# Output weights of a scan made over two temporaries in an idle buffer, with their loads first in the queue and new planner seeds

## The chip, the cores and the metric

The kernel runs on one core of one Trainium2 chip. The metric is device time in microseconds (us). Before the change three runs took 769.33, 770.93 and 770.23 us, a median of 770.23 us. A core has five engines that are named here as in the profile: PE (matrix multiply; PEld is its weight load), ACT (activation functions), DVE (vector), POOL (GpSimd) and SP, which only issues DMAs. Each engine runs its own list of instructions in order, and they wait for each other through semaphores.

## The reference, cut to what matters

Two branches, whose results stand side by side in the output (2048 rows, 640 + 640 columns).

```python
# A: a diagonal complex state-space scan
dt = jnp.exp(log_dt)
Lam_bar = jnp.exp(dt * Lam)
B_bar = ((Lam_bar - 1.0) / Lam)[:, None] * Bmat
Bu = jnp.einsum("bld,pd->blp", x + 0j, B_bar)
for t in range(L):
    h = Lam_bar[None, :] * h + Bu[:, t, :]
y = 2.0 * jnp.einsum("blp,dp->bld", hseq, Cmat).real + x * Dskip
# B: attention with 32 query heads of 20 columns over one key and one value head
scores = jnp.einsum("bhqd,bkd->bhqk", q, k) * (Dh ** -0.5)
p = softmax(scores, axis=-1)
out = jnp.einsum("bhqk,bkd->bhqd", p, v) @ wo
```

S = L = 2048, D = P = 640.

## The kernel before

**Attention sets the pace.** The 2048 query rows are four blocks of 512, the 32 heads go in groups of four, so there are 32 groups. A group needs its scores against 16 key chunks for each of four heads: 64 units of 128 keys x 512 query columns, 2048 units in all. A unit goes one of two ways. Either PE writes its scores into one of two large PSUM tiles, `R0` (three units) or `R1` (two units), and one ACT instruction (L1263, here "an exp") takes two or three units at a time to `P`; or PE writes them into a single bank, and DVE approximates the exponential in integers: one conversion (L1269) and three shifted copies (L1274) over up to three units at once (here "a D unit"). PE then multiplies the exponentials with the values into `PV`, DVE takes a finished group out (`OTr`, L1307), SP stores it to `o_rows`. Four times, after eight groups, `dense_ops` reads a whole block back into `OTd`, POOL multiplies it by the softmax denominators, and PE projects it with `WO4`. A group takes at most 16 D units (`QUOTA`).

**The scan runs in between.** It has four blocks of 512 rows and five chunks of 128 states, 20 scan units. For each, PE multiplies the input (`xaT`) with `BTre` and `BTim`, DVE rotates the result (`tm0` to `tm3`, L901), POOL adds it up (`uh`, L917), DVE runs the recurrence (`hh`, L928), POOL rotates back (`tm4` to `tm7`) and adds up into `W`. When the five chunks of a block are there, `y_tile` multiplies `W` with the output weights `CGre` and `CGim`.

**The output weights** are C scaled per state by a complex factor that is made on the chip: for each of the five chunks and each of re and im, POOL makes a product in five pieces of 128 columns in the temporary `ctmp` (L858), and DVE makes the other product and the sum in one instruction (L860). C arrives by transposing DMAs into buffers that are idle so far: chunks 0 to 3 lie in `W`, chunk 4 in `ostage`. `ctmp` lies in `tm4` to `tm6`. So the way back of the scan, which writes `tm4` to `tm7`, is gated until all ten weights are made (`prog["c"]`).

**A planner sets the order.** Nothing is ordered by hand after the set-up: at build time `main` keeps the remaining operations in named threads (`sc` holds what precedes the scan, its DMAs among it; `sa`, `su`, `sr`, `sy` are the scan; `sx` loads `xaT` of the later blocks), offers the head of every thread beside the next exp, fill, D unit and so on, and issues what can begin first by the planner's own durations, with small random choices. The choices are varied over 64 equal stretches of the 2048 units, each with a seed from `SEEDS` (0 is a seed like another). The order that comes out is fixed in the program: each engine runs its list, and an instruction that waits holds up everything behind it on its engine. A gate is tested when the planner issues, not on the chip; there only semaphores wait.

Of the kernel before, what the change touches and what calls it, by code (L numbers as in the profile page):

```python
# [9 lines left out]
ALU = mybir.AluOpType  # L10
AX = mybir.AxisListType
FP32 = mybir.dt.float32
# [231 lines left out]
class _Kernel:  # L244
    S, D, H, DH = 2048, 640, 32, 20
    NC, NQB, NKC, NGG = 5, 4, 16, 8
# [18 lines left out]
    SEEDS = (19006, 20002, 21006, 22006, 23001, 24003, 25001, 26002, 27008, 28003, 0, 30006, 31008, 32005, 33006,  # L265
# [28 lines left out]
    def alloc(self):  # L294
        S, NC = self.S, self.NC
# [66 lines left out]
        self.ctmp = self.tm[:].rearrange("p i n -> p (i n)").bitcast(FP32)[:, 1024:1664]  # L362
# [454 lines left out]
    def scan_ops(self):  # L817

        K, NC = self, self.NC
        sc, NGRE, NGIM, GRE, GIM = K.sc, self.NGRE, self.NGIM, self.GRE, self.GIM  # L820
        t = self.t
        sa, su, sr, sy, sc_ = [], [], [], [], []
        self.prog = prog = dict(x=0, a=0, u=0, s=0, r=0, y=0, w=0, c=0)
# [9 lines left out]
        ct = [f"tm{i}{h}" for i in (4, 5, 6) for h in self.PIECES]  # L833
# [14 lines left out]
        for c in range(NC):  # L848
            for i, nm in ((0, "cre"), (1, "cim")):
                sc_.append(self.dma(K.Craw[c][:, i, :], t[nm][:, 128 * c:128 * (c + 1)], f"craw{c}{i}",  # L850
                                    writes=[f"Craw{c}{i}"] + ([f"ostage{i}"] if c == 4 else []), tr=True, kb=160))
        for c in range(NC):
            cr, ci = K.Craw[c][:, 0, :], K.Craw[c][:, 1, :]
            keys = [f"Craw{c}0", f"Craw{c}1", "sc"] + (["ostage0", "ostage1"] if c == 4 else ws)
            for (dst, x, y, gx, gy, op, nm) in ((K.CGre, cr, ci, GRE, GIM, ALU.subtract, "CGre"),
                                                (K.CGim, ci, cr, NGRE, NGIM, ALU.add, "CGim")):
                for i in range(0, 640, 128):
                    pool(lambda e, y=y, c=c, gy=gy, i=i: e.tensor_scalar(K.ctmp[:, i:i + 128], y[:, i:i + 128], sc[:, gy, c:c + 1],  # L858
                                                                         None, op0=ALU.mult), keys, [f"ct{i}"] + ct * (i == 0), 128)
                dve(lambda e, dst=dst, x=x, op=op, c=c, gx=gx: e.scalar_tensor_tensor(  # L860
                    out=dst[:, c, :], in0=x, scalar=sc[:, gx, c:c + 1], in1=K.ctmp, op0=ALU.mult, op1=op),
                    keys + ct + [f"ct{i}" for i in range(0, 640, 128)], [nm], 695)
        sc_[-1].done = lambda: prog.update(c=1)
        for b in range(4):
# [3 lines left out]
            if b < 3:  # L868
                pool = mk(su, "pool")
# [10 lines left out]
        sx = [o for b in (1, 2, 3) for o in self.load_xa(b, lambda b=b: prog["y"] >= 4 * (b - 1), lambda b=b: prog.update(x=b))]  # L880
        return sc_, sy, sr, su, sa, sx
# [649 lines left out]
```

## Time and profile before

The profiled execution took 770.28 us, of which 768.6 us are the span from the first to the last instruction; 1.7 us lie around it.

| engine | busy us | share of the span |
|---|---|---|
| PE | 704.8 | 92% |
| DVE | 708.3 | 92% |
| ACT | 752.5 | 98% |
| POOL | 446.0 | 58% |

Busy time is the union of an engine's instructions; neighbours on ACT and DVE overlap, so the mean length of one instruction is longer than the distance between two. A row of a group of instructions shows the source line, the engine, the operation, what is written and read with its shape, the count, then busy us and mean ns, then the idle time of the engine before them and what ended it. A row of the timeline begins with start and length in us.

### The profile page before, as it was taken

The page shows a single profiled execution, that of the slowest core. Times are in us where ns is not written, and L with a number is a line of the kernel's source. Part 1 is how long each engine was busy: PE and PEld are TensorE (multiplying, and loading weights), DVE is VectorE, ACT ScalarE, POOL GpSimd, SP SyncE. Part 2 cuts the span into 40 slices and gives each one's busy share as a digit, 9 for nine tenths or more (in the row PEclk, how much of TensorE's full clock was granted, in tenths as well). Part 3 has the DMA queues.
Part 4 walks back from the last instruction along what each step waited for, and adds up shares of the span by engine and source line. Part 5 has one row for each costly group of instructions (what it writes and reads, how often), then busy time and mean ns, then how long its engine had stood idle before and what let it go on. Part 6 is the DMA issues. An engine that isn't in the chain of part 4 may idle for free.

```text
span 768.6 us, 16664 instructions
## 1 busy us (share of the span) xinstructions
PE 704.8 (92%) x6538; PEld 213.4 (28%) x6538; DVE 708.3 (92%) x1236; ACT 752.5 (98%) x710; POOL 446.0 (58%) x867
## 2 busy tenths in 40 slices
PE   5799988888889999998889999988889999889998
PEld 2222222222222333322223323322223332223333
DVE  5599999999998999999997999999999789999986
ACT  8999999999999999999999999999999999999995
POOL 5612354579989931088997300199986469990040
PEclk9899999899999999999999999999999999999999
DMA  9366301000021100220002100040000201000020
GB/s 186 57 143 134 74 16 49 8 24 14 3 51 30 42 8 27 56 60 15 15 9 67 42 23 9 23 93 10 15 15 28 66 33 34 14 15 17 18 61 35
DMA packets 61179, 31.50 MB, mean 41 GB/s; under 512 B 41510, under 2 KB 61102, under 8 KB 61102
## 3 DMA queue, kind: packets, MB, share of 16 engines
q1 hardware_dynamic: 59606, 30.14, 15.9%
q8 instruction: 52, 0.85, 0.5%
q10 hardware_dynamic: 1496, 0.30, 0.2%
q14 instruction: 25, 0.20, 0.1%
HBM read 9.21 MB, written 12.69 MB: 28 GB/s over the span
## 4 chain that ended last, share of the span: by engine, by line
ACT 74%; PE 15%; DVE 9%; POOL 1%; DMA 1%; issue 1%; ACTq 0%; DVEq 0%; POOLq 0%
ACT P L1263 72%; PE R L421 5%; PE PV L421 5%; PE B L421 4%; DVE Pd L1274 4%; DVE Pd L1269 3%; DVE hh L928 1%; DVE tm L901 1%; POOL tm L858 1%; DMA WO<-in_B_wk_dram 1%; ACT cs L691 1%; ACT Pd L690 0%; ACT KT L538 0%; DVE CGre L860 0%; ACT L503 0%
## 5 line engine op out<-in xcount | busy, mean ns | idle before, releaser
L1263 ACT ACTIVATE P<-R 128x1024 bf16<-128x1024 f32 (+1 forms) x677 | 733.1, 1354 | 4.3 <-PE R L421 1.8
L421 PE MATMUL R<-QT,KT 32*128 32x512 bf16 (+1 forms) x1685 | 266.9, 389 | 48.6 <-ACT P L1263 37.1
L1269 DVE TENSOR_SCALAR Pd<-B 128x512 int16<-128x512 f32 x363 | 245.5, 682 | 19.4 <-PE B L421 17.0
L1274 DVE TENSOR_SCALAR Pd<-Pd 128x1536 int16<-128x1536 int16 (+2 forms) x513 | 260.2, 541 | 0.4
L421 PE MATMUL PV<-Pd,VP 128*32 128x512 bf16 x1744 | 256.9, 386 | 2.0 <-DVE OTr L1307 1.0
L421 PE MATMUL PV<-P,VP 128*32 128x512 bf16 x1612 | 253.3, 389 | 0.7 <-DVE OTr L1307 0.6
L917 POOL TENSOR_TENSOR tm<-hh,cs 128x128 bf16<-128x128 f32 x320 | 163.9, 533 | 17.7 <-DVE hh L928 8.3
L421 PEld LDWEIGHTS R<-QT,KT 32*128 32x128 bf16 (+1 forms) x1685 | 66.1, 91 | 301.0 <-ACT P L1263 271.0
L421 PE MATMUL B<-QT,KT 32*128 32x512 bf16 x363 | 141.0, 389 | 0.0
L917 POOL TENSOR_TENSOR uh<-tm 128x128 bf16<-128x128 bf16 x160 | 81.0, 527 | 97.6 <-DVE tm L901 93.7
L917 POOL TENSOR_TENSOR W<-tm 128x128 bf16<-128x128 bf16 x160 | 93.5, 608 | 49.4 <-PE B L421 45.3
L421 PEld LDWEIGHTS PV<-Pd,VP 128*32 128x32 bf16 x1744 | 60.1, 94 | 65.7 <-issue 40.5
L421 PEld LDWEIGHTS PV<-P,VP 128*32 128x32 bf16 x1612 | 58.1, 94 | 58.8 <-issue 46.6
L1011 POOL TENSOR_TENSOR OTd<-OTd,rwide 128x128 bf16<-128x128 bf16 x80 | 33.2, 443 | 60.0 <-DMA OTd<-o_rows 58.2
L1269 DVE TENSOR_SCALAR Pd<-R 128x512 int16<-128x512 f32 x73 | 49.9, 683 | 3.0 <-PE R L421 2.4
L901 DVE TENSOR_TENSOR tm<-B,cs 128x1024 bf16<-128x1024 f32 x40 | 48.5, 1213 | 1.0 <-PE B L421 0.6
L858 POOL TENSOR_SCALAR tm<-W,sc 128x128 f32<-128x128 bf16 x40 | 32.3, 821 | 27.5 <-DVE CGre L860 15.9
L421 PE MATMUL B<-CGre,W 128*128 128x384 bf16 (+1 forms) x160 | 46.4, 305 | 0.0
L421 PE MATMUL B<-CGim,W 128*128 128x384 bf16 (+1 forms) x160 | 45.5, 299 | 0.0
L928 DVE TENSOR_TENSOR_SCAN hh<-sc,hini,uh 128x512 f32<-128x512 f32 x30 | 40.7, 1358 | 0.0
L421 PEld LDWEIGHTS B<-QT,KT 32*128 32x128 bf16 x363 | 32.9, 91 | 0.0
L421 PE MATMUL B<-xaT,BTre 128*128 128x512 bf16 x100 | 30.1, 384 | 0.1
(149 smaller groups left out, 437.2 us busy)
## 6 DMA issues: line engine op xcount, KB each, us to landing
o_rows<-OTr SPq DMA_DIRECT2D x32, 128.0 KB, 1.7
QT<-q_rows SPq DMA_DIRECT2D x30, 128.0 KB, 2.2
q_rows<-Qd SPq DMA_DIRECT2D x16, 160.0 KB, 2.9
OTd<-o_rows SPq DMA_DIRECT2D x16, 160.0 KB, 3.4
out_dram<-ystage SPq DMA_DIRECT2D x16, 160.0 KB, 1.9
out_dram<-ostage SPq DMA_DIRECT2D x12, 160.0 KB, 1.8
P<-in_B_wq_dram SPq DMA_DIRECT2D x1, 800.0 KB, 5.6
WO<-in_B_wo_dram SPq DMA_DIRECT2D x4, 200.0 KB, 3.4
```

The source lines that it names most:

```text
L421: ins = e.matmul(o() if callable(o) else o, lhsT=l, rhs=r, start=st, stop=sp, skip_group_check=True, **kw)
L691: act(lambda e, c=c, b=b: e.activation(K.cs[:, c, :, :].rearrange("p i n -> p (i n)"), K.tri[:, 4 * b + 2:4 * b + 4, :].rearrange("p r n - ...
L858: pool(lambda e, y=y, c=c, gy=gy, i=i: e.tensor_scalar(K.ctmp[:, i:i + 128], y[:, i:i + 128], sc[:, gy, c:c + 1], None, op0=ALU.mult), key ...
L901: dve(lambda e, k=k, h=h: e.tensor_tensor(K.tm[:, 2 * k:2 * k + 2, :], bass.AP(tensor=K.BB, offset=512 * int(h.key[1]), ap=[[512 * self.BA ...
L917: put(lambda e, c0=c0, end=end: e.tensor_tensor(out[:, c0:end], a[:, c0:end], b[:, c0:end], op), reads, [writes + h], n, gate=None if i el ...
L928: dve(lambda e, ri=ri, ini=ini: e.tensor_tensor_scan(K.hh[:, ri, :], dec, K.uh[:, ri, :], ini, ALU.mult, ALU.add), ["sc", *(f"uh{ri}{h}" f ...
L1011: ops.append(Op("pool", lambda e, c=c, m=m: e.tensor_tensor(K.OTd[:, m, c], K.OTd[:, m, c], K.rwide[:, c], ALU.mult), rw + [f"OTe{dd}" for ...
L1263: return Op("act", lambda e: e.activation(dst, K.R[n % 2][:, 0:512 * size], ACT.Exp, scale=self.exp_scale), [f"R{n % 2}"] + ["R0c"] * (siz ...
L1269: return Op("dve", lambda e: e.tensor_scalar(K.Pd[:, 0, u, :], K.B[x][:, :], self.d_off, 0.0, op0=ALU.add, op1=ALU.max), [key], [f"Pd{u}_0 ...
L1274: return Op("dve", lambda e: e.tensor_scalar(K.Pd[:, i, a:b, :], K.Pd[:, 0, a:b, :], float(self.SHIFTS[i]), 0.0, op0=ALU.subtract, op1=ALU ...
```

## The change

- `ctmp` becomes two temporaries of 640 columns in `OTd`, one for re and one for im; before, one lay in `tm4` to `tm6`.
- The ten transposing loads of C are a thread of their own, `sl`, put ahead of `sc` in the list of threads and in the code ahead of the loads of `WO4`.
- The POOL pieces (`sk`) and the DVE instructions (`sg`) of the weights are threads of their own as well. Gates let POOL issue the pieces of weight n when weight n-2 has been issued on DVE and its chunk's loads have been issued, and DVE issue weight n after its five pieces.
- The gate `prog["c"]` moves: the scan's way back may write `tm4` to `tm7` at any time; the writes into `W` and the first `dense_ops` wait for it instead, since C lies in `W` and the temporaries lie in `OTd`.
- The loads of `xaT` of later blocks are gated by three issued weights as well.
- All 64 seeds are replaced.

```diff
-        self.ctmp = self.tm[:].rearrange("p i n -> p (i n)").bitcast(FP32)[:, 1024:1664]
+        self.ctmp = self.OTd[:].rearrange("p c n -> p (c n)").bitcast(FP32).rearrange("p (i n) -> p i n", i=2)
...
+        for c in range(NC):
+            for i, nm in ((0, "cre"), (1, "cim")):
+                sl.append(self.dma(K.Craw[c][:, i, :], t[nm][:, 128 * c:128 * (c + 1)], f"craw{c}{i}",
+                                   writes=[f"Craw{c}{i}"] + ([f"ostage{i}"] if c == 4 else []), tr=True, kb=160,
+                                   done=(lambda c=c: prog.update(l=c + 1)) if i else None))
...
+                for i in range(0, 640, 128):
+                    pl(lambda e, y=y, c=c, gy=gy, i=i, h=h: e.tensor_scalar(K.ctmp[:, h, i:i + 128], y[:, i:i + 128], sc[:, gy, c:c + 1],
+                                                                            None, op0=ALU.mult), keys, [f"ct{h}{i}"], 128,
+                       gate=lambda n=2 * c + h: prog["g"] >= n - 1 and prog["l"] > n // 2, done=(lambda n=2 * c + h + 1: prog.update(k=n)) if i == 512 else None)
+                cd(lambda e, dst=dst, x=x, op=op, c=c, gx=gx, h=h: e.scalar_tensor_tensor(
+                    out=dst[:, c, :], in0=x, scalar=sc[:, gx, c:c + 1], in1=K.ctmp[:, h, :], op0=ALU.mult, op1=op),
+                    keys + [f"ct{h}{i}" for i in range(0, 640, 128)], [nm] + [f"OTd{i}{j}" for i in range(NC) for j in self.PIECES] * (c == NC - 1), 695,
+                    gate=lambda n=2 * c + h: prog["k"] > n, done=lambda n=2 * c + h + 1: prog.update(g=n, c=int(n == 2 * NC)))
...
-                   gate=lambda: prog["s"] > u and prog["c"], done=(lambda: prog.update(r=u + 1)) if i == 3 else None)
-        free = lambda: prog["y"] >= 4 * b
+                   gate=lambda: prog["s"] > u, done=(lambda: prog.update(r=u + 1)) if i == 3 else None)
+        free = lambda: prog["y"] >= 4 * b and prog["c"]
```

Both programs are lists of instructions that can be laid side by side without a run. They are the same up to the first fills of `R0`. Behind that the order differs on every engine, and these counts differ:

```
                                   before   after
ACT  exp of two units                 419     391
ACT  exp of three units               258     280
DVE  conversion of a D unit           436     426
DVE  shifted copy, 3 units            354     333
DVE  shifted copy, 2 units             87      96
DVE  shifted copy, 1 unit              77      92
PE   R<-QT,KT and B<-QT,KT           2048    2048
PE   PV<-P,VP                        1612    1622
PE   PV<-Pd,VP                       1744    1704
PE   PV<-cs,VP (multiplies zeros)      72      79
```

Counted in units filled on PE, the first multiplication with `CGre` stands behind 679 units before and 473 after, the last behind 2004 and 1812. On DVE's list the ten weights stand behind 32, 43, 46, 55, 59, 66, 69, 75, 81 and 84 D units before, and behind 18, 25, 26, 27, 27, 28, 31, 34, 41 and 45 after.

Between the second and the seventh of the weights, DVE's list after the change reads (a "conversion" is that of a D unit, `tm` is the scan's rotation):

```
CGim chunk 0; OTr; conversion; CGre chunk 1; conversion; tm; CGim chunk 1; shifted copy x3 units;
CGre chunk 2; conversion; tm; CGim chunk 2; shifted copy x3 units; Qd; conversion;
shifted copy x3 units; conversion x2; CGre chunk 3
```

and POOL's list beside it: the five pieces for `CGim` of chunk 1, five for `CGre` of chunk 2, five for `CGim` of chunk 2, two for `CGre` of chunk 3, five `uh` pieces of the scan, the other three for `CGre` of chunk 3. The first pieces for `CGim` of chunk 1 wait for `CGim` of chunk 0 on DVE, which reads the same temporary.

On SP's list the four stores of the first `Qd` block stand right behind the last load of `BTim`, the ten loads of C follow, with the store of `Gs`, the first store of `OTr` and two loads of `QT` between the second and the fourth of them; the eight loads of `WO4` and the next block of `xaT` stand behind them. Before, the loads of C came last of all these.

More of the change, by code (lines that the diff above doesn't have):

```diff
@@ L832, in scan_ops @@
         ws = self.w_keys = [f"W_{c}{r}{h}" for c in range(NC) for r in "ri" for h in self.PIECES]
-        ct = [f"tm{i}{h}" for i in (4, 5, 6) for h in self.PIECES]
         dve, pool = mk(sc_, "dve"), mk(sc_, "pool")
         self.post_constants(dve, pool)
-        old = ["wk4", "wk_raw", "wv_raw", "onesrow", "selrow"] + ["veclim", "vecldt", "veclre", "vecdsk"]
+        for c in range(NC):
[3 more added lines that the diff above has]
+                                   done=(lambda c=c: prog.update(l=c + 1)) if i else None))
+        old = ["wk4", "wk_raw", "wv_raw", "onesrow", "selrow"] + ["veclim", "vecldt", "veclre", "vecdsk"]
+        sk, sg = [], []
+        pl, cd = mk(sk, "pool"), mk(sg, "dve")
+        for c in range(NC):
+            cr, ci = K.Craw[c][:, 0, :], K.Craw[c][:, 1, :]
+            keys = [f"Craw{c}0", f"Craw{c}1", "sc"] + (["ostage0", "ostage1"] if c == 4 else ws)
+            for (dst, x, y, gx, gy, op, nm) in ((K.CGre, cr, ci, GRE, GIM, ALU.subtract, "CGre"),
+                                                (K.CGim, ci, cr, NGRE, NGIM, ALU.add, "CGim")):
+                h = int(nm == "CGim")
+                for i in range(0, 640, 128):
[6 more added lines that the diff above has]
+                    gate=lambda n=2 * c + h: prog["k"] > n, done=lambda n=2 * c + h + 1: prog.update(g=n, c=int(n == 2 * NC)))
         for i in range(2):
@@ L847, in scan_ops @@
                 sc_.append(self.dma(dst, src, f"wo{j}{w}", reads=["WO4"], writes=[f"WO4_{j}{w}"], kb=200 if w else 50))
[L848 to L863, printed above, removed]
         for b in range(4):
@@ L879, in scan_ops @@
                 self.y_tile(sy, mk(sy, "dve"), b, q)
[L880 to L881 removed]
+        sx = [o for b in (1, 2, 3) for o in self.load_xa(b, lambda b=b: prog["y"] >= 4 * (b - 1) and prog["g"] > 2, lambda b=b: prog.update(x=b))]
+        return sl, sc_, sk, sg, sy, sr, su, sa, sx
     def load_xa(self, b, gate=None, done=None):
@@ L981, in dense_ops @@
         ops = []
-        have = lambda: all(g in self.normed for g in range(self.NGG * qb, self.NGG * qb + (6 if qb == self.NQB - 1 else 8))) and (
+        have = lambda: self.prog["c"] and all(g in self.normed for g in range(self.NGG * qb, self.NGG * qb + (6 if qb == self.NQB - 1 else 8))) and (
             qb == 0 or qb - 1 in self.projected)
```

10 lines of the change are left out of this document (5 added, 5 removed), and 8 rows, old and new, of the table SEEDS.

## The prediction

> **What bounds the kernel now.** I read the page first, then ACT's groups, ACT's timeline, the stretches in which it loses time, and what DVE and POOL do there.
>
> ```profile
> span 768.6 us, 16664 instructions
> PE 704.8 (92%) x6538; PEld 213.4 (28%) x6538; DVE 708.3 (92%) x1236; ACT 752.5 (98%) x710; POOL 446.0 (58%) x867
> ```
>
> Three engines are above 90%, but only ACT is nearly gapless. What matters is the distance from one exp to the next when nothing holds ACT up, and how many exps there are. From ACT's groups, and from four windows of the exps' line (form counts behind first and last start):
>
> ```profile
> L1263 ACT ACTIVATE P<-R 128x1024 bf16<-128x1024 f32 x419 | 457.8, 1189 | 1.1 <-PE R L421 0.7 <-PE B L421 0.2
> L1263 ACT ACTIVATE P<-R 128x1536 bf16<-128x1536 f32 x258 | 418.3, 1621 | 3.2 <-PE R L421 1.2 <-PE B L421 1.1 <-PE PV L421 0.6
> ...
> L1263 ACT ACTIVATE P<-R x7: 1167/1180/1188, 92.7 to 98.2; 128x1024 bf16<-128x1024 f32 x7
> L1263 ACT ACTIVATE P<-R x108: 1017/1328/1767, 147.4 to 262.8; 128x1024 bf16<-128x1024 f32 x67, 128x1536 bf16<-128x1536 f32 x41
> ...
> L1263 ACT ACTIVATE P<-R x27: 1017/1067/1544, 21.7 to 51.6; 128x1024 bf16<-128x1024 f32 x16, 128x1536 bf16<-128x1536 f32 x11
> L1263 ACT ACTIVATE P<-R x87: 1017/1217/1758, 53.3 to 145.8; 128x1024 bf16<-128x1024 f32 x57, 128x1536 bf16<-128x1536 f32 x30
> ```
>
> The two busy times add up to more than the span, so the means are no prices. Seven exps of two units start over 5.5 us: 5.5 / 6 = 0.917 us each. In the second window 107 exps take 115.4 us; with 66 or 67 of two units, one of three takes 1.34 to 1.35 us, and I use 1.34. ACT's timeline gives the ends of its unbroken runs:
>
> ```profile
> 21.68 2.37 ACT L1263 ACTIVATE P<-R 128x1536 bf16<-128x1536 f32 x2
> 24.62 9.21 ACT L1263 ACTIVATE P<-R 128x1536 bf16<-128x1536 f32 x8 [0.58 <-PE R L421]
> 34.45 18.72 ACT L1263 ACTIVATE P<-R 128x1536 bf16<-128x1536 f32 x17 [0.62 <-PE PV L421]
> 53.34 90.51 ACT L1263 ACTIVATE P<-R 128x1024 bf16<-128x1024 f32 x85 [0.17 <-PE B L421]
> 144.32 2.54 ACT L1263 ACTIVATE P<-R 128x1536 bf16<-128x1536 f32 x2 [0.46 <-PE B L421]
> 147.45 12.81 ACT L1263 ACTIVATE P<-R 128x1536 bf16<-128x1536 f32 x12 [0.60 <-PE R L421]
> ...
> 753.71 5.33 ACT L1263 ACTIVATE P<-R 128x1536 bf16<-128x1536 f32 x5
> ```
>
> So the span splits into 21.7 us before the first exp, 737.4 us of exps (21.68 to 759.04), and 9.6 us behind them. The exps alone would take 419 x 0.917 + 258 x 1.34 = 729.9 us; ACT loses 7.4 us among them. By stage: from 21.68 to 53.34 the 27 exps need 16 x 0.917 + 11 x 1.34 = 29.4 of 31.7 us, a loss of 2.2; from 53.34 to 147.45 the 87 need 92.5 of 94.1, a loss of 1.6; the remaining 563 need 608.1 of 611.6, a loss of 3.5. **ACT's own work sets the time**; everything else can matter only through these 7.4 us, or through new ones.
>
> **The exps.** The instruction lists of both programs show that the changed one leaves ten units more to ACT: 28 fewer exps of two, 22 more of three. That is 22 x 1.34 - 28 x 0.917 = 29.5 - 25.7 = **+3.8 us**, and 3.6 to 4.1 with 1.33 to 1.35 for three. No engine hides it, since ACT has next to no idle time to put it in. DVE is relieved of ten D units:
>
> ```profile
> L1269 DVE TENSOR_SCALAR Pd<-B 128x512 int16<-128x512 f32 x363 | 245.5, 682 | 19.4 <-PE B L421 17.0
> L1274 DVE TENSOR_SCALAR Pd<-Pd 128x1536 int16<-128x1536 int16 x354 | 205.5, 608 | 0.2
> L1274 DVE TENSOR_SCALAR Pd<-Pd 128x1024 int16<-128x1024 int16 x87 | 35.8, 450 | 0.2
> L1274 DVE TENSOR_SCALAR Pd<-Pd 128x512 int16<-128x512 int16 x72 | 20.9, 323 | 0.1
> L901 DVE TENSOR_TENSOR tm<-B,cs 128x1024 bf16<-128x1024 f32 x40 | 48.5, 1213 | 1.0 <-PE B L421 0.6
> L1307 DVE CAST OTr<-PV 128x512 bf16<-128x512 f32 x32 | 21.9, 686 | 3.9 <-PE PV L421 3.3
> L775 DVE TENSOR_SCALAR Qd<-B 128x512 bf16<-128x512 f32 x20 | 13.7, 684 | 1.3 <-PE B L421 1.0
> L860 DVE SCALAR_TENSOR_TENSOR CGre<-W,sc,tm 128x640 bf16<-128x640 bf16 x4 | 3.5, 876 | 0.5 <-POOL tm L858 0.5
> ```
>
> 10 x 0.682 for conversions, and 21 x 0.608 - 9 x 0.450 - 15 x 0.323 = 3.9 for shifted copies, some 11 us; what DVE doesn't do in this way becomes idle time, not speed.
>
> **The making of the weights.** The number of POOL pieces and DVE instructions stays (50 and 10). What they cost before shows on POOL and in one place on DVE and PE:
>
> ```profile
> L858 POOL TENSOR_SCALAR tm<-W,sc 128x128 f32<-128x128 bf16 x40 | 32.3, 821 | 27.5 <-DVE CGre L860 15.9
> L917 POOL TENSOR_TENSOR uh<-tm 128x128 bf16<-128x128 bf16 x160 | 81.0, 527 | 97.6 <-DVE tm L901 93.7
> ...
> 75.77 3.05 POOL L858 TENSOR_SCALAR tm<-W,sc 128x128 f32<-128x128 bf16 x5
> 133.74 5.32 POOL L858 TENSOR_SCALAR tm<-W,sc 128x128 f32<-128x128 bf16 x5 [3.33 <-DVE CGim L860]
> ...
> 139.19 0.89 DVE L860 SCALAR_TENSOR_TENSOR CGre<-W,sc,tm 128x640 bf16<-128x640 bf16 x1 [0.52 <-POOL tm L858]
> ...
> 139.61 0.40 PE L421 MATMUL PV<-P,VP 128*32 128x512 bf16 x3
> 140.83 0.61 PE L421 MATMUL R<-QT,KT 32*128 32x512 bf16 x3 [0.81 <-DVE Pd L1269]
> ...
> 120.00:141.00 21.00, 17.13 (x179) 4.49 (x179) 19.96 (x38) 21.00 (x20) 13.86 (x16) 0.92 0.17 44
> 141.00:149.00 8.00, 7.97 (x59) 1.58 (x55) 7.16 (x14) 6.88 (x7) 2.78 (x5) 0.58 0.06 19
> ```
>
> POOL waited for DVE (27.5 us), which costs nothing at 58% busy. Only once did DVE wait for POOL, 0.52 us at 139.19, behind pieces that had taken 5.32 us. PE then waited 0.81 us for a conversion that was queued behind, the granted clock fell to 0.58 in the next 8 us, its matmuls went from 0.40 to 0.61 us, and ACT lost its 0.46 and 0.60 us there. I put the whole loss of this stage, 1.6 us, to this wait, and take it out: **-1.6 us** (0 if the new plan loses as much for another reason).
>
> With two temporaries the waiting turns round. In the new lists, from the end of CGim of chunk 0 to CGre of chunk 3, DVE has four weights, one OTr, one Qd, two tm, three shifted copies of three units and six conversions: 4 x 0.876 + 0.686 + 0.684 + 2 x 1.213 + 3 x 0.608 + 6 x 0.682 = 13.2 us. POOL must put 20 pieces and five uh into the same time, and none can begin before that end, since the first writes the temporary just read. At 3.05 / 5 = 0.61 us a piece that is 12.2 + 2.6 = 14.8 us, at the mean of 0.821 it is 19.1 us. **DVE waits 1.6 to 5.9 us there**, in three or four places, with conversions and scan rotations queued behind it, and PE's banks and fills behind those. The planner can't see this: it reckons a piece at 128 / 450 + 0.1 = 0.384 us (L827), so by its count POOL is ready in time.
>
> The first weight may wait as well:
>
> ```profile
> 51.23 1.28 SPq L402 DMA_TRANSPOSE BTim<-in_A_B_im_dram  x1
> 54.26 2.64 SPq L404 DMA_DIRECT2D q_rows<-Qd  x4
> ...
> W<-in_A_C_im_dram SPq DMA_TRANSPOSE x4, 2.9
> ...
> 51.82 0.69 DVE L1307 CAST OTr<-PV 128x512 bf16<-128x512 f32 x1 [0.21 <-PE PV L421]
> ```
>
> SP is done with BTim at 52.5; four stores bring it to 55.2, two transposes (1.27 us of issue each, as for BTim) to 57.7, the second lands 2.9 us later, and five pieces make it 64 to 65. DVE, after OTr at 52.5, first meets a Qd that overwrites what the four stores read, so it stands still until they land, at about 58 by the same 2.9 us; PE goes on with the fills for the exps meanwhile, which need no DVE. With five conversions, the Qd and two shifted copies (5.2 us) it is at CGre of chunk 0 at some 63 us: a wait of up to 2 us more.
>
> What does such a wait cost ACT? From below nothing: DVE's 19.4 us of waits for PE's banks cost at most a part of the 7.4. From above 1.6 / 0.52, three times its length. The wait before is the nearest row, but most of its price was the clock, which is paid once for several waits close together, and pieces run at their short length while DVE stands still. So I take 3 us of DVE waits and a little less than that on ACT: **+2.5 us**, with 0 and three times the middle of the waits, 3 x 3.75 = 11, as ends.
>
> The Trainium skill (TensorE: Matmul & The Clock Gate, "HAM oscillation") says that the clock is halved after PE pauses of more than about 3.4 us. This trace disagrees: the pause of 0.81 us, in a stretch with PE 82% busy, went ahead of a clock of 0.58. By the rule the new waits would cost no clock, and with them hidden the sum would be that of the second rival.
>
> **Moved DMAs and buffers: 0.** C's ten loads take SP 12.7 us, now ahead of WO4's and the next xaT's; two QT loads stay near 62 us (65 before), and need is not sooner. The first block's five scan units cover the later xaT; without that cover the scan would start its second block some 10 us later, and it ends 192 units earlier than before. OTd is first read from memory long after the last weight:
>
> ```profile
> L404 SPq DMA_DIRECT2D OTd<-o_rows x16: 316/436/465, 226.7 to 736.9; - x16
> ```
>
> What stands ahead of the first exp is the same list, and what follows the last one consists of the same instructions; I carry both, and the losses of 2.2 and 3.5 us in the other stages.
>
> **Sum.** 770.28 + 3.8 - 1.6 + 2.5 = **775.0 us**; the profiled time is the median of 770.23 within 0.1 us.
>
> **Rivals.** *Nothing is lost after the start-up* (not slower): the scan runs 200 units earlier, DVE has slack, and no exp waits behind 53 us. Then 770.28 + 3.8 - 1.6 - 3.5 = 769.0 us. It decides once the losses fall by more than 3.8 in all. For it speaks that DVE is 11 us freer; against it that the 3.5 us are spread over 560 exps, with no single cause to remove. *The waits are hidden*: PE has enough fills ahead of DVE, the clock holds, and only the exps' count counts: 770.28 + 3.8 - 1.6 = 772.5 us. Against it stands the 0.52 us wait, which was not hidden. *The waits are paid threefold* as at 139 us: 772.5 + 11 = 784 us; it needs the clock to fall several times. *The change doesn't do what it says*, POOL still waiting for DVE each time: then no new wait, and again 772.5.
>
> **How the numbers follow.** Forecast (773 to 779) 0.50; hidden, or not doing what it says, 0.20; nothing lost 0.16; threefold (above 779) 0.14. About 0.2%, or 1.5 us, is what a measurement can tell from no change: 768.7 to 771.8 is the same. Of the third case half falls below 768.7, and another 0.02 from a better start-up: faster 0.10. The other half, and some of the hidden waits with smaller losses: same 0.14. Slower 0.76. The range is 769.0 to 781.0; the forecast's own is 773 to 779.
>
> **What would show it.** Right: 391 and 280 exps at unchanged distances; the waits of the weights' DVE line for POOL grow from 0.5 to 3 us or more, between 60 and 110 us; a granted clock below 1 there; POOL's waits for DVE at that line shrink. Wrong: ACT's loss among the exps below 4 us, or DVE waits of several us with an unbroken ACT.

## The result and the profile after

| kernel | median us | runs | lowest to highest |
|---|---|---|---|
| before | 769.8 | 4 | 769.33 to 770.93 |
| after | 782.53 | 4 | 782.14 to 783.56 |

The ratio is 1.0168, with a 95% interval from 1.0147 to 1.0188: the changed kernel is slower by 12.7 us, where 4.7 were forecast. The profiled execution took 782.81 us, 781.0 of them the span. Its page shows the busy times, and below them the shares of the chain of work that ended last:

```profile
span 781.0 us, 16543 instructions
PE 687.8 (88%) x6452; PEld 211.9 (27%) x6515; DVE 704.8 (90%) x1229; ACT 757.3 (97%) x704; POOL 439.9 (56%) x867
...
ACT 70%; POOL 12%; DVE 9%; PE 8%; issue 1%; POOLq 0%; ACTq 0%; DVEq 0%
ACT P L1267 68%; POOL OTd L850 4%; DVE Pd L1278 3%; POOL tm L921 3%; PE R L421 3%; DVE Pd L1273 3%; PE B L421 3%; POOL uh L921 2%; PE PV L421 2%; POOL W L921 2%; DVE hh L932 1%; DVE tm L905 1%; ACT cs L691 1%; DVE Qd L775 0%; ACT Pd L690 0%
```

In this kernel the exps have line 1267, the conversions 1273, the shifted copies 1278, the weights 850 (POOL) and 853 (DVE), the scan's POOL work 921. POOL is busy for 56% of the span as before, and yet 12% of the last chain are its own: 4% are the weights' pieces, 7% the scan's `tm`, `uh` and `W`. A share of the span can't show that; it has to be looked at where it falls. First ACT, by groups and then by its timeline (start, length, count; the idle time before is in brackets):

```profile
L1267 ACT ACTIVATE P<-R 128x1536 bf16<-128x1536 f32 x280 | 452.4, 1616 | 9.2 <-PE R L421 5.1 <-PE B L421 3.0 <-PE PV L421 0.6
L1267 ACT ACTIVATE P<-R 128x1024 bf16<-128x1024 f32 x391 | 436.4, 1194 | 3.5 <-PE B L421 1.9 <-PE R L421 1.4
```

```profile
21.04 2.41 ACT L1267 ACTIVATE P<-R 128x1536 bf16<-128x1536 f32 x2
...
43.65 40.48 ACT L1267 ACTIVATE P<-R 128x1536 bf16<-128x1536 f32 x38 [0.28 <-PE B L421]
86.08 2.37 ACT L1267 ACTIVATE P<-R 128x1536 bf16<-128x1536 f32 x2 [1.95 <-PE R L421]
89.23 8.72 ACT L1267 ACTIVATE P<-R 128x1536 bf16<-128x1536 f32 x8 [0.78 <-PE B L421]
99.16 4.68 ACT L1267 ACTIVATE P<-R 128x1536 bf16<-128x1536 f32 x4 [1.21 <-PE R L421]
104.66 11.41 ACT L1267 ACTIVATE P<-R 128x1536 bf16<-128x1536 f32 x10 [0.82 <-PE B L421]
116.99 16.13 ACT L1267 ACTIVATE P<-R 128x1536 bf16<-128x1536 f32 x14 [0.93 <-PE R L421]
133.47 3.71 ACT L1267 ACTIVATE P<-R 128x1536 bf16<-128x1536 f32 x3 [0.35 <-PE B L421]
138.00 1.02 ACT L1267 ACTIVATE P<-R 128x1024 bf16<-128x1024 f32 x1 [0.81 <-PE B L421]
139.19 12.89 ACT L1267 ACTIVATE P<-R 128x1536 bf16<-128x1536 f32 x11 [0.17 <-PE R L421]
152.66 1.02 ACT L1267 ACTIVATE P<-R 128x1024 bf16<-128x1024 f32 x1 [0.58 <-PE B L421]
154.30 2.39 ACT L1267 ACTIVATE P<-R 128x1536 bf16<-128x1536 f32 x2 [0.61 <-PE B L421]
157.28 23.65 ACT L1267 ACTIVATE P<-R 128x1024 bf16<-128x1024 f32 x21 [0.59 <-PE R L421]
...
749.16 22.52 ACT L1267 ACTIVATE P<-R 128x1024 bf16<-128x1024 f32 x20
```

The exps run from 21.04 to 749.16 + 22.52 = 771.68, which is 750.6 us. At the prediction's distances they need 391 x 0.917 + 280 x 1.34 = 733.7, so ACT now loses 16.9 us among them, 9.5 more than before. With the +3.8 of the exps that is +13.3; an earlier first exp (0.6) and a slightly shorter end (some 0.2) leave about +12.5, the difference of the spans. And the place is narrow: between 84.13 and 157.28 the brackets hold 8.8 us, where before 1.2 us stood between 53 and 161. After that ACT goes on as before. What the engines did in that place stands in the stretches, with the granted clock behind the busy times, of after (with a short stretch of its own, for later, ahead of them) and then of before:

```profile
84.00:91.00 7.00, 4.76 (x46) 1.30 (x46) 6.28 (x10) 4.26 (x5) 6.69 (x11) 1.00 0.11 31
86.00:110.00 24.00, 18.29 (x167) 4.91 (x170) 21.73 (x33) 21.10 (x19) 22.72 (x36) 0.93 0.02 7
110.00:141.00 31.00, 24.15 (x225) 6.59 (x220) 26.73 (x38) 28.64 (x26) 29.48 (x55) 1.00 0.13 35
141.00:160.00 19.00, 15.55 (x138) 4.26 (x140) 18.38 (x30) 17.20 (x16) 18.09 (x36) 0.91 0.03 9
```

```profile
86.00:110.00 24.00, 22.42 (x216) 5.80 (x208) 23.95 (x40) 24.00 (x25) 12.11 (x19) 1.00 0.13 23
110.00:141.00 31.00, 24.82 (x259) 6.50 (x259) 29.96 (x55) 31.00 (x29) 18.05 (x22) 0.94 0.12 31
141.00:160.00 19.00, 18.00 (x152) 4.28 (x148) 17.93 (x36) 17.88 (x17) 9.31 (x12) 0.82 0.03 9
```

The columns are PE, PEld, DVE, ACT, POOL, clock. POOL went from 12.1 to 22.7 of 24 us, from 18.1 to 29.5 of 31 and from 9.3 to 18.1 of 19: over these 74 us it is the busiest engine. PE and DVE do less than before on the whole, and the clock isn't to blame: by these rows a lower clock took 3.4 us from PE (24 x 0.07 + 19 x 0.09) where it took 5.3 before (31 x 0.06 + 19 x 0.18). How POOL's lateness reaches ACT is read from the timeline of POOL, DVE and PE, and its sum from the view of DVE's waits (total us, times, longest):

```profile
75.78 12.65 POOL L850 TENSOR_SCALAR OTd<-W,sc 128x128 f32<-128x128 bf16 x17 [5.23 <-DVE CGim L853]
...
83.35 0.89 DVE L853 SCALAR_TENSOR_TENSOR CGre<-W,sc,OTd 128x640 bf16<-128x640 bf16 x1 [2.38 <-POOL OTd L850]
...
84.89 0.82 PE L421 MATMUL B<-xbT,wqd 128*128 128x512 bf16 x3 [2.51 <-DVE Pd L1273]
...
88.79 0.39 PE L421 MATMUL R<-QT,KT 32*128 32x512 bf16 x3 [1.34 <-DVE Qd L775]
...
92.36 0.94 DVE L853 SCALAR_TENSOR_TENSOR CGre<-W,sc,OTd 128x640 bf16<-128x640 bf16 x1 [1.46 <-POOL OTd L850]
...
114.00 0.89 DVE L853 SCALAR_TENSOR_TENSOR CGre<-ostage,sc,OTd 128x640 bf16<-128x640 bf16 x1 [1.50 <-POOL OTd L850]
...
136.19 1.22 DVE L905 TENSOR_TENSOR tm<-B,cs 128x1024 bf16<-128x1024 f32 x1 [2.03 <-POOL uh L921]
```

```profile
DVE CGre L853 <- POOL OTd L850: 5.3, 3, 2.4
...
DVE tm L905 <- POOL uh L921: 2.0, 1, 2.0
...
DVE CGim L853 <- POOL OTd L850: 0.6, 1, 0.6
```

POOL can't begin before `CGim` of chunk 0 has read the shared temporary (75.7 us) and works with next to no pause from then on. DVE arrives at `CGre` of chunk 2 and stands for 2.38 us. The conversion behind it is late, PE waits 2.51 us for the bank that it empties, the fill of `R` stands behind that on PE's list, and ACT idles 1.95 us at 84.13. The same repeats for the later weights, and at 136 DVE waits for the scan's `uh`, which POOL does after the last pieces. In all DVE waits 8.0 us for POOL; before it was 0.5 us.

### The profile page after: what moved, and what is told of

Same layout as the page of the kernel before. It is cut to its first block, busy times and chain, and to the rows that moved or that the text cites. A ratio compares the mean times of both kernels' runs of the same rounds, so it can differ in the third digit from the quotient of the medians.

```text
span 781.0 us, 16543 instructions
## 1 busy us (share of the span) xinstructions
PE 687.8 (88%) x6452; PEld 211.9 (27%) x6515; DVE 704.8 (90%) x1229; ACT 757.3 (97%) x704; POOL 439.9 (56%) x867
## 4 chain that ended last, share of the span: by engine, by line
ACT 70%; POOL 12%; DVE 9%; PE 8%; issue 1%; POOLq 0%; ACTq 0%; DVEq 0%
ACT P L1267 68%; POOL OTd L850 4%; DVE Pd L1278 3%; POOL tm L921 3%; PE R L421 3%; DVE Pd L1273 3%; PE B L421 3%; POOL uh L921 2%; PE PV L421 2%; POOL W L921 2%; DVE hh L932 1%; DVE tm L905 1%; ACT cs L691 1%; DVE Qd L775 0%; ACT Pd L690 0%
## 5 line engine op out<-in xcount | busy, mean ns | idle before, releaser
L1273 DVE TENSOR_SCALAR Pd<-B 128x512 int16<-128x512 f32 x374 | 253.2, 682 | 22.7 <-PE B L421 19.7
L421 PE MATMUL PV<-P,VP 128*32 128x512 bf16 x1622 | 257.3, 388 | 0.6 <-DVE Pd L1273 0.5
L421 PE MATMUL PV<-Pd,VP 128*32 128x512 bf16 x1704 | 252.0, 387 | 3.9 <-DVE Pd L1278 1.6
L421 PE MATMUL B<-QT,KT 32*128 32x512 bf16 x374 | 144.8, 387 | 0.0
L921 POOL TENSOR_TENSOR W<-tm 128x128 bf16<-128x128 bf16 x160 | 89.0, 579 | 31.0 <-PE B L421 27.1
L850 POOL TENSOR_SCALAR OTd<-W,sc 128x128 f32<-128x128 bf16 x40 | 29.6, 753 | 24.0 <-DMA W<-in_A_C_im_dram 17.6
L1273 DVE TENSOR_SCALAR Pd<-R 128x512 int16<-128x512 f32 x52 | 35.6, 684 | 3.6 <-PE R L421 3.4
L421 PE MATMUL B<-xbT,wqd 128*128 128x512 bf16 x88 | 26.4, 386 | 4.2 <-DVE Pd L1273 3.0
```

The costliest lines, as they stand in the source:

```text
L421: ins = e.matmul(o() if callable(o) else o, lhsT=l, rhs=r, start=st, stop=sp, skip_group_check=True, **kw)
L850: pl(lambda e, y=y, c=c, gy=gy, i=i, h=h: e.tensor_scalar(K.ctmp[:, h, i:i + 128], y[:, i:i + 128], sc[:, gy, c:c + 1], None, op0=ALU.mult ...
L921: put(lambda e, c0=c0, end=end: e.tensor_tensor(out[:, c0:end], a[:, c0:end], b[:, c0:end], op), reads, [writes + h], n, gate=None if i el ...
L1273: return Op("dve", lambda e: e.tensor_scalar(K.Pd[:, 0, u, :], K.B[x][:, :], self.d_off, 0.0, op0=ALU.add, op1=ALU.max), [key], [f"Pd{u}_0 ...
```

## The experiments

**1. Take the new work off POOL.** In the changed kernel all 50 pieces write 16 of their 128 columns, and DVE's instruction reads the first 16 again and again; number and order of the instructions stay.

```diff
-    e.tensor_scalar(K.ctmp[:, h, i:i + 128], y[:, i:i + 128], sc[:, gy, c:c + 1],
+    e.tensor_scalar(K.ctmp[:, h, i:i + 16], y[:, i:i + 16], sc[:, gy, c:c + 1],
...
-    out=dst[:, c, :], in0=x, scalar=sc[:, gx, c:c + 1], in1=K.ctmp[:, h, :], op0=ALU.mult, op1=op),
+    out=dst[:, c, :].rearrange("p (r n) -> p r n", n=16), in0=x.rearrange("p (r n) -> p r n", n=16), scalar=sc[:, gx, c:c + 1],
+    in1=bass.AP(tensor=K.OTd, offset=1280 * h, ap=[[2560, 128], [0, 40], [1, 32]]).bitcast(FP32), op0=ALU.mult, op1=op),
```

> The changed kernel in its own order on every engine, but each of the 50 POOL pieces works on 16 of its 128 columns, and DVE reads those 16 columns forty times over; the rest of the weights' products is left out. POOL theory (the changed kernel loses 16 us of ACT time because POOL's pieces take longer than the planner reckons and DVE waits 6.0 us for them): the 6.0 us of DVE waits at the weights' line go to under 1 us, ACT's loss between 75 and 160 us falls from about 10 us to under 4, and the time to 773 to 777 us. Rival (order theory: the new seeds put PE's fills late in that stage, whatever POOL does): the waits go, the time stays at 780 to 783. Clock theory (the loss is the halved granted clock): time falls only as far as the two half-clock spells at 101 and 152 us vanish, to about 780.

Measured: 773.35 us, a ratio of 1.0040 [1.0018, 1.0062]. So 9 of the 12.7 us hang on the length of the pieces, and what is left, some 3 us, is about the exps' term. The stretch from 75 to 161 us, after the change and then with short pieces:

```profile
75.00:161.00 86.00, 67.06 (x591) 18.40 (x596) 76.27 (x111) 77.07 (x69) 81.06 (x140) 0.96 0.15 36
75.00:161.00 86.00, 76.36 (x677) 20.41 (x669) 85.36 (x129) 85.20 (x78) 73.72 (x142) 1.00 0.16 41
```

ACT idles 0.8 us there instead of 8.9. The order of the instructions can't be the cause of these 9 us, since it is the same in both. Nor can the clock alone: it rose from 0.96 to 1.00, but in the same stretch before the change it was 0.94, and ACT lost little there. Nor did the long pieces hold up DVE's own work: its 27 shifted copies of three units between 55 and 130 us took 628 ns in the mean after the change and 662 here. (The profiled execution took 779.7 us, seven others 772.7 to 774.6; in it DVE's `Qd` had to wait 3.6 us for the stores of the `Qd` before it. Only its waits for POOL are used here.)

**2. The same in the kernel before.**

```diff
-    e.tensor_scalar(K.ctmp[:, i:i + 128], y[:, i:i + 128], sc[:, gy, c:c + 1],
+    e.tensor_scalar(K.ctmp[:, i:i + 16], y[:, i:i + 16], sc[:, gy, c:c + 1],
...
-    out=dst[:, c, :], in0=x, scalar=sc[:, gx, c:c + 1], in1=K.ctmp, op0=ALU.mult, op1=op),
+    out=dst[:, c, :].rearrange("p (r n) -> p r n", n=16), in0=x.rearrange("p (r n) -> p r n", n=16), scalar=sc[:, gx, c:c + 1],
+    in1=bass.AP(tensor=K.tm, offset=2048, ap=[[4096, 128], [0, 40], [1, 32]]).bitcast(FP32), op0=ALU.mult, op1=op),
```

> The kernel before in its own order, with the same shortening of the 50 POOL pieces (16 of 128 columns each). If the one DVE wait of 0.52 us for POOL cost the 1.6 us that ACT lost between 53 and 147 us, as the prediction took it, the time falls by 1 to 1.6 us, to 768.2 to 768.9. Rival: the loss there had another cause (the transfer of a finished group, the fill's own place in PE's list), and the time stays within 0.5 us of the kernel before.

Measured: 769.1 us over 10 runs, a ratio of 0.9998 [0.9985, 1.0011]. Its ACT timeline shows that the stage which the prediction blamed is mended:

```profile
53.03 127.54 ACT L1264 ACTIVATE P<-R 128x1024 bf16<-128x1024 f32 x119 [0.18 <-PE B L421]
```

There is no break at 144 and 147 any more. But the medians don't show it: the interval allows a gain of 1.2 us at most, not 1.6. The loss was there in the one profiled execution, and its removal isn't worth what that profile priced it at. Perhaps it isn't there in every execution: of the 16 of the kernel before that stand beside this run, seven took 768.1 to 769.0 us, about as long as the profiled 768.41 of this one. No profile shows what those seven did.

**3. Exchange the seeds.** Each kernel with the other's 64 seeds, all else unchanged.

```diff
-    SEEDS = (19006, 20002, 21006, 22006, 23001, 24003, 25001, 26002, 27008, 28003, 0, 30006, 31008, 32005, 33006,
+    SEEDS = (23004, 24009, 25009, 26001, 27005, 28009, 29003, 30007, 31009, 32005, 33003, 34006, 35006, 36002,
...
```

> The kernel before with the 64 new seeds alone. Its exps are 409 of two units and 271 of three, 738.2 us by the distances 0.917 and 1.34, 8.3 us more than before. Theory that the weights' new making costs through POOL: nothing is lost beyond what was before, so 770 + 8 = 778 us, with at most 1 us of DVE waits for POOL. Rival (seeds alone make the loss among the exps): ACT's loss grows from 7 to 12 us or more, and the time is 783 or more.

> The changed kernel with the 64 old seeds. Its exps are 444 of two units, 245 of three and one of one unit, 735.9 us, 6 us more than the kernel before. POOL theory: DVE waits 4 us or more for POOL at the weights' line here too, since the planner reckons a piece at 0.384 us whatever the seeds, and ACT loses 12 us or more among the exps: 781 to 787 us. Rival (the new seeds made the loss): DVE waits under 2 us, loss near 7 us, 776 us.

Measured: 797.15 us (1.0352 [1.0325, 1.0379]) for the old weights with the new seeds, 793.96 us (1.0310 [1.0280, 1.0340]) for the new weights with the old. They are 27 and 24 us slower than before, where 778 and 781 to 787 us were expected. Seeds are choices along one course of planning; as soon as the structure differs they are 64 arbitrary numbers. So the times of these two runs say what unsearched seeds cost, and nothing on the share of the seeds in this change; experiment 6 puts that question better. One thing does carry over: DVE waits 7.5 us for POOL with the new weights and 0.4 with the old ones, so the waits come with the two temporaries and the freer order, under either set of seeds.

**4. Which of the weights?** Short pieces, as in 1, for some of the ten only.

```diff
+        cut = lambda n: 16 if 3 <= n <= 6 else 128
...
-    e.tensor_scalar(K.ctmp[:, h, i:i + 128], y[:, i:i + 128], sc[:, gy, c:c + 1],
+    e.tensor_scalar(K.ctmp[:, h, i:i + cut(2 * c + h)], y[:, i:i + cut(2 * c + h)], sc[:, gy, c:c + 1],
```

`short_mid` has weights 4 to 7 short as shown, `short_late` weights 8 to 10 (`n >= 7`), `short_early` weights 1 to 3 (`n <= 2`).

> The changed kernel in its own order; only the pieces of the fourth to the seventh weight (CGim of chunk 1 to CGre of chunk 3) work on 16 of 128 columns, the rest of their products is left out. Price-by-wait theory (each DVE wait costs its own loss): the waits of 4.5 us at 83 to 92 us go, and with them the 5.2 us that ACT lost between 86 and 105 us; the wait of 1.5 us at 114 and the losses from 117 to 160 us (5.1 us) stay: 777 us. Backlog theory (POOL is behind by some 10 us once, and passes it on to the later weights and to the scan's uh, until it has caught up): these losses go as well, 773 to 774 us.

> The changed kernel in its own order; only the pieces of the last three weights (CGim of chunk 3, CGre and CGim of chunk 4) work on 16 of 128 columns, the rest of their products is left out. Price-by-wait theory: the wait of 1.5 us at 114 us goes and 1.0 us of ACT's loss with it, 781.5 us. Backlog theory: the 4.5 us of waits before stay with their loss of 5.2 us, but 15 pieces of 0.5 us less let POOL catch up before the scan's uh at 134 us, so the losses from 117 to 160 us (5.1 us) go: 777 to 778 us.

> The changed kernel in which only the pieces of the first three weights (15 of 50) write 16 of their 128 columns, and the sum of these weights reads those 16 columns again and again, so that three weights are wrong; all else is as in the changed kernel. It stands beside the runs in which weights 4 to 7 (a ratio to before of 1.0122) and 8 to 10 (1.0140) were short; all ten short gave 1.0040 and none 1.0168. My theory: GpSimd is late only from the end of CGim of chunk 0 on (75.7 us), since before that it has done all 15 pieces and waits 5.2 us for that instruction. Making these 15 pieces shorter then only lengthens that wait: a ratio of 1.015 to 1.019, with the weights' waits of DVE for POOL still 5 us or more. Rival one: every piece costs the same wherever it stands; then 15 of 50 pieces take off 0.3 of 0.0128, a ratio of 1.013. Rival two: the shares of the three parts add up; then the first three weights must hold what the other two runs left, 0.0128 - 0.0046 - 0.0028 = 0.0054, a ratio of 1.0114.

Measured: 777.75 us (1.0122 [1.0107, 1.0137]), 779.23 us (1.0140 [1.0123, 1.0157]) and 780.64 us (1.0137 [1.0109, 1.0165]). In `short_mid` the waits behind `CGim` of chunk 0 fall from 4.5 to 0.2 us and the time to what was expected if each wait has its own price (777), not to the 773 to 774 of a backlog that is passed on: the ninth weight still waits 2.3 us, and ACT still idles 3.9 us between 111 and 152 us. `short_late` keeps most of the waits up to 93 us and loses the later ones; its ACT timeline, and DVE's waits:

```profile
87.32 2.53 ACT L1271 ACTIVATE P<-R 128x1536 bf16<-128x1536 f32 x2 [3.16 <-PE R L421]
...
104.92 22.70 ACT L1271 ACTIVATE P<-R 128x1536 bf16<-128x1536 f32 x20 [0.85 <-PE B L421]
127.81 4.62 ACT L1271 ACTIVATE P<-R 128x1536 bf16<-128x1536 f32 x4 [0.18 <-PE B L421]
132.65 46.99 ACT L1271 ACTIVATE P<-R 128x1536 bf16<-128x1536 f32 x42 [0.22 <-PE B L421]
```

```profile
DVE CGre L857 <- POOL OTd L854: 4.6, 3, 2.4
...
DVE tm L909 <- POOL uh L925: 0.4, 1, 0.4
```

From 104.92 to 179.64 ACT idles 0.4 us, where the changed kernel idled 4.0 us from 116.07 to 157.28. So those losses, behind the ninth weight and on into the scan, hang on the pieces of the last three weights. (The wait for `uh` fell from 2.0 to 0.4 us in `short_mid` and `short_early` as well, so it proves nothing by itself.) The time lies between the two theories' 777 to 778 and 781.5: neither holds alone. `short_early` answers by POOL's timeline and DVE's waits:

```profile
74.51 12.65 POOL L854 TENSOR_SCALAR OTd<-W,sc 128x128 f32<-128x128 bf16 x17 [7.27 <-DVE CGim L857]
```

```profile
DVE CGre L857 <- POOL OTd L854: 6.5, 4, 2.4
...
DVE tm L909 <- POOL uh L925: 0.4, 1, 0.4
```

The time that POOL saved on the first 15 pieces only lengthened its wait for `CGim` of chunk 0 from 5.23 to 7.27 us; the 17 pieces behind take the same 12.65 us, and DVE waits as long as before or longer. That is what the theory said. The time isn't as clear: its interval holds the theory's lower end, rival one's 1.013 and, just, rival two's 1.0114.

**5. The length of a piece.** Once 64 of 128 columns in every piece, of which DVE reads the first 64 for the whole width (its part of the edit is as in experiment 1 and isn't shown), once all 128 with temporaries in bf16.

```diff
-    e.tensor_scalar(K.ctmp[:, h, i:i + 128], y[:, i:i + 128], sc[:, gy, c:c + 1],
+    e.tensor_scalar(K.ctmp[:, h, i:i + 64], y[:, i:i + 64], sc[:, gy, c:c + 1],
```

```diff
-        self.ctmp = self.OTd[:].rearrange("p c n -> p (c n)").bitcast(FP32).rearrange("p (i n) -> p i n", i=2)
+        self.ctmp = self.OTd[:].rearrange("p c n -> p (c n)")[:, 0:1280].rearrange("p (i n) -> p i n", i=2)
```

> The changed kernel in its own order, with all 50 pieces on 64 of their 128 columns (DVE reads those 64 columns ten times; the rest of the products is left out). A piece should take about 0.35 us instead of 0.60, below the 0.384 us that the planner reckons. If what matters is whether POOL keeps the pace that the planner reckons, nearly all of the 9 us goes: 773 to 775 us, DVE waits under 1 us. If the loss is in proportion to POOL's time for the pieces (16 columns: 773.4, 128 columns: 782.5), it ends at about 777 to 778 us.

> The changed kernel in its own order, complete, but with the two temporaries in bf16 instead of float32, so the products are rounded once more. If POOL's 0.60 us for a piece comes from writing float32, a piece falls to about 0.4 us, near the planner's 0.384, and the time to 774 to 777 us. Rival: the price is that of the operation with a scalar per partition, whatever it writes; then a piece stays at 0.6 us and the time at 782.

Measured: 774.88 us (1.0068 [1.0043, 1.0093]) and 783.04 us (1.0168 [1.0129, 1.0207]). The view of the pieces' line gives shortest, median and longest duration in ns; for 16 columns, for 64, and for 128 in bf16:

```profile
L850 POOL TENSOR_SCALAR OTd<-W,sc x40: 321/327/1416, 62.9 to 98.8; 128x16 f32<-128x16 bf16 x40
```

```profile
L850 POOL TENSOR_SCALAR OTd<-W,sc x40: 439/445/1472, 60.3 to 94.0; 128x64 f32<-128x64 bf16 x40
```

```profile
L850 POOL TENSOR_SCALAR OTd<-W,sc x40: 599/605/1598, 60.6 to 99.0; 128x128 bf16<-128x128 bf16 x40
```

The steps are (445 - 327) / 48 = 2.46 and (605 - 445) / 64 = 2.50 ns a column, so 0.29 us of an instruction are there before its first column; the planner's count is 0.1 us and 2.22 ns. So half a piece is slower than the planner's 0.384 us; the time came out at 773 to 775 all the same, with 2.4 us of DVE waits where under 1 was expected, 0.86 of them at the first weight, before the stage in question. The type of the result changes nothing, neither in the piece nor in the time.

**6. Mend it.** First, a whole weight's product in one instruction; four one-column memsets of an unused tile stand in for the other four pieces, so that the list stays the same. Nothing is left out.

```diff
-    pl(lambda e, ...: e.tensor_scalar(K.ctmp[:, h, i:i + 128], y[:, i:i + 128], sc[:, gy, c:c + 1],
-                                      None, op0=ALU.mult), keys, [f"ct{h}{i}"], 128,
+    pl((lambda e, ...: e.tensor_scalar(K.ctmp[:, h, :], y, sc[:, gy, c:c + 1], None, op0=ALU.mult)) if i == 512
+       else (lambda e, k=4 * (2 * c + h) + i // 128: e.memset(K.junk[:, k:k + 1], 0.0)), keys, [f"ct{h}{i}"], 128,
```

> The changed kernel in its own order, complete: the first four of a weight's five POOL instructions only clear a column of an unused tile, and the fifth makes the product for all 640 columns. From pieces of 0.327, 0.445 and 0.605 us for 16, 64 and 128 columns a POOL instruction costs 0.29 us and 2.47 ns a column, so a weight should take 4 x 0.10 + 0.29 + 640 x 0.00247 = 2.3 us instead of 3.0; the planner reckons 1.9. Pace theory: the waits fall to about 2 us in all and the time to 775 to 777 us. Rival: one instruction of 1.9 us stands in the way of DVE's shifted copies for longer than five short ones, and what is gained on POOL is lost on DVE: 780 us or more.

Measured: 775.16 us, a ratio of 1.0077 [1.0053, 1.0102]. The groups and DVE's wait:

```profile
L851 POOL TENSOR_SCALAR OTd<-W,sc 128x640 f32<-128x640 bf16 x8 | 16.9, 2112 | 0.2
```

```profile
DVE CGre L854 <- POOL OTd L851: 0.7, 1, 0.7
```

2.11 us instead of five pieces of 0.60 or more: the waits fall to 0.7 us and the time by 7 us. That doesn't make it as fast as before.

Second, the planner reckons a piece at 225 / 450 + 0.1 = 0.60 us, and the seeds are searched again, with equal effort, for the new weights and for the old.

```diff
-    None, op0=ALU.mult), keys, [f"ct{h}{i}"], 128,
+    None, op0=ALU.mult), keys, [f"ct{h}{i}"], 225,
```

> The changed kernel, planned with 0.60 us for a piece of the weights (225 columns in place of 128 in the planner's formula), and with 64 seeds chosen again, one stretch after the other, by the end that the planner reckons. Its exps are 419 of two, 262 of three and one of one unit: 735.8 us, 5.9 more than before. Price theory: with the right price the waits for POOL go below 1.5 us even with two temporaries, ACT loses about 8 us as before, and the time is 776 to 779 us. Rival: POOL is simply too slow for the weights beside the scan, DVE waits 3 us or more and ACT loses 12 us or more: 781 us or more.

> The kernel before with the same price of 0.60 us for a piece and 64 seeds chosen in the same way and with the same effort. Its exps are 441 of two, 243 of three and two of one unit: 731.0 us, 1.1 more than before. If the two temporaries do no harm or good by themselves, the loss among the exps is within 3 us of that of the other run with this price, and the time follows the exps: 4 to 5 us less than it. Rival: with one temporary the scan starts later and ACT loses more, so that it ends at the same time or later.

Measured: 782.01 us (1.0167 [1.0142, 1.0192]) and 780.99 us (1.0174 [1.0129, 1.0219]). The first was expected at 776 to 779 us, the second 4 to 5 us below it; both expectations failed. DVE waits 3.9 us for POOL with the new weights and not at all with the old ones, but by the distances above ACT loses 14.8 and 15.2 us among its exps, and of the 14.8 only 3.8 lie between 53 and 161 us. With the same price and the same search the two ways of making the weights can't be told apart in time; both lose to the kernel before, whose seeds serve it better than this search's, which found another seed than 0 for only ten of the 64 stretches. How much of the 12.7 us would be left to the new weights after a search as good as that one stays open, and no version that beats the kernel before was found.

**All runs with the changed kernel's list of instructions, side by side.** The second column is the sum of DVE's waits for POOL in the profiled execution, at the weights and at the scan's `tm`; the third is the ratio's excess over 1 times 769.8.

| kernel | DVE waits for POOL, us | slower than before, us |
|---|---|---|
| all pieces short | 0.6 | 3.1 |
| one wide piece | 0.7 | 5.9 |
| half pieces | 2.4 | 5.2 |
| weights 4 to 7 short | 4.1 | 9.4 |
| weights 8 to 10 short | 5.6 | 10.8 |
| temporaries in bf16 | 7.0 | 12.9 |
| weights 1 to 3 short | 7.5 | 10.5 |
| after | 8.0 | 12.9 |

A straight line through the eight has 3.7 us at no wait, and 1.15 us more for each us of waiting (standard errors 0.9 and 0.17; the points lie up to 1.8 us off it). The first number agrees with the exps' term, the second is the price of a wait, roughly: the waits are those of one execution each. A line through the other seven alone gives 12.9 us for the changed kernel. The wide piece and the half pieces show what the line leaves out: in both, ACT's breaks of 2.6 us stand in or right behind a spell of half clock, from 124.4 to 131.2 us in the one and 124.7 to 131.6 in the other, with no wait of DVE for POOL beside them.

## Why the prediction was wrong

The direction was right, and DVE waited for POOL where it was expected to; the time lies above the range because the sizes of two terms were wrong, and the second of them also left out the waits that came later.

**The exps, +3.8: right.** Counts and distances are as forecast, and the row of the longest unbroken run agrees:

```profile
L1267 ACT ACTIVATE P<-R x38: 1018/1242/1711, 43.6 to 83.0; 128x1024 bf16<-128x1024 f32 x25, 128x1536 bf16<-128x1536 f32 x13
```

25 x 0.917 + 13 x 1.34 = 40.35 us, and the run took 40.48. The straight line of the experiments has 3.7 us where DVE waits for nothing.

**The old weights' stage, -1.6: at most 1.2 of it.** The prediction put the whole loss between 53 and 147 us of one execution to one wait of 0.52 us. Experiment 2 shows that the breaks behind it vanish in the profile, and that the medians don't move by as much. So between 0.4 us and the whole 1.6 us of the error lie here.

**The new waits, +2.5: the step that failed, by its size.** In the stretch that the prediction named, DVE waits 2.38 + 0.62 + 1.46 = 4.5 us, within its 1.6 to 5.9. But it wrote "So I take 3 us of DVE waits and a little less than that on ACT". Three things are wrong with it. The 3 us lie below the middle of its own bounds, on the ground that pieces run at their short length while DVE stands still. They do, but others ran beside DVE's work and were longer (last section), and 4.5 us came of it. The stretch ended at the seventh weight, while POOL was late on through the ninth (1.50 us) and into the scan (2.03 us at 136): the prediction counted 20 pieces and five `uh`, and didn't ask what POOL had to do next. That is 8.0 us of waits instead of 3. And the price was put below one because "most of its price was the clock, which is paid once". The largest break came without it: in the stretch from 84 to 91 us ACT was busy for 4.26 of 7 us at a granted clock of 1.00. A wait of DVE was passed on to ACT at about 1.15 us a us, since conversions stand behind the weights on DVE and fills of `R` behind the conversions' banks on PE. 8.0 x 1.15 = 9.2 us stand against the 2.5, and 769.8 + 3.7 + 9.2 = 782.7. PE's pauses after the change bear on the rule that the prediction weighed. PE waited 2.51 us in one piece at 82.4, and the clock stayed at 1.00. That agrees with the Trainium skill (TensorE: Matmul & The Clock Gate, "HAM oscillation"), by which it takes pauses of more than some 3.4 us to halve it. The pause of 0.81 us before the change, ahead of 0.58, still disagrees, and so do two after it: the clock was 0.50 from 100.7 and from 151.9 us, for 3.4 us each, behind pauses of at most 1.49 and 0.76 us in the 3.4 us before. What sets these spells off stays open.

**The moved DMAs, 0: not measured by itself.** The first weight began at 63.5 us without a wait, near the forecast of 63 to 65, and ACT ran unbroken past the place where DVE met the `Qd` stores. Neither is sure, though. In the profiled executions of half pieces, `bf16_temporaries` and experiment 4, with the same order, DVE waited 0.4 to 1.8 us for POOL at the first weight, whose pieces wait for the loads of C; the table's sums include that. And in the one execution of experiment 1 where the wait was 3.6 us, the time was 779.7 instead of some 773 us. No run undid the move of the loads alone.

**The rivals.** The time came out where the threefold rival stood (784, with a chance of 0.14), but not by its mechanism: the waits were longer than its 3.75 us, the price about one, and the clock was no lower than before. It did fall at 100.7 us, as the prediction foresaw, and again at 151.9, and 2.6 of ACT's 8.8 us stand in those two spells or right behind them (the breaks before 104.66, 152.66, 154.30 and 157.28); how much of that is the clock's own stays open. The two cheap rivals fall with the rows above. The change does what it says: POOL's waits for DVE ahead of the pieces fell from 36.3 us to 5.2.

## What to carry to other kernels

An engine at 56% over the whole span can be the bound of a stretch of 75 us; when work is moved into a shorter time, reckon the busy share of that time, at the measured price, and follow the backlog until that engine has caught up. Where an in-order engine feeds the pace-setter through others without slack, reckon about a us of the end for each us of its waiting, as here. And a term that was read from one break in one execution is worth no more than the spread of the runs.

## What the runs showed of the hardware

**A piece on POOL takes longer beside some of DVE's instructions.** Of the 50 pieces of the changed kernel, 31 took 595 to 604 ns and 19 took 816 to 1660 ns. Each of the 19 overlaps for at least 0.34 us with a DVE instruction that reads only SBUF: a shifted copy, a weight or the scan's recurrence `hh`. Beside conversions, `OTr` and the rotation, which read PSUM, a piece keeps its 0.60 us; so do five pieces during which DVE began a weight's instruction, in its first half. Two pieces and their neighbours, from the timeline of both engines:

```profile
117.01 1.01 DVE L1278 TENSOR_SCALAR Pd<-Pd 128x1536 int16<-128x1536 int16 x2
117.01 1.41 POOL L850 TENSOR_SCALAR OTd<-ostage,sc 128x128 f32<-128x128 bf16 x1
...
118.17 1.23 DVE L905 TENSOR_TENSOR tm<-B,cs 128x1024 bf16<-128x1024 f32 x1
...
118.90 0.60 POOL L850 TENSOR_SCALAR OTd<-ostage,sc 128x128 f32<-128x128 bf16 x1
```

The first piece took 0.81 us longer than the second, within the 1.01 us of the two shifted copies. The Trainium skill (SBUF — State Buffer, "SBUF: two separate sides") has a rule for it: DVE, in some of its modes or with two inputs from SBUF, and GpSimd share a pair of ports that one instruction holds until its end while the other is blocked. The rows agree for POOL. For DVE they don't show it: the five weights' instructions that began during a piece took 0.89 to 0.99 us, where the shortest of the ten took 0.87. So the mean of 0.821 us in the profile before was the price of pieces that stood beside DVE's SBUF work (24 of the 50 pieces then took longer than 0.70 us, 23 of them beside such an instruction for 0.26 us or more), and the 17 pieces behind `CGim` of chunk 0 took 12.65 / 17 = 0.74 us each, between the prediction's 0.61 and 0.82.
